# Block-granular projection items and a cost budget for interleaving them, in a cross-shaped window attention kernel

## The chip, the cores and the metric

The kernel runs on one core of one Trainium2 chip. The metric is the device time of one execution, in microseconds (us), as a median of several.

Engine names: PE is TensorE, ACT is ScalarE, DVE is VectorE, SP is the engine that issues most DMAs (all but three of those listed for the kernel before). "PEld" in profile lines is PE's weight load, which overlaps its matmuls (in the kernel before 575.6 us of it and 1049.5 us of matmuls lie in a span of 1307.2 us).

## The reference, cut to what matters

```python
qkv = einsum('bhwc,cd->bhwd', x, wqkv)           # x: 1 x 224 x 224 x 96, bf16
q, k, v = qkv[..., :96], qkv[..., 96:192], qkv[..., 192:]
# channels 0..47:  attention inside 28 horizontal windows, each 8 rows  x 224 columns
# channels 48..95: attention inside 28 vertical windows,   each 224 rows x 8 columns
ah = softmax(einsum('bqc,bkc->bqk', qh, kh) * 48 ** -0.5)
oh = einsum('bqk,bkc->bqc', ah, vh)              # and the same for qv, kv, vv
return einsum('bhwc,cd->bhwd', concat(oh, ov), wo)
```

There are 56 windows of 1792 tokens each, with head size 48. Phase one of the kernel does the 28 horizontal windows and phase two the vertical ones. Phase two also transposes and projects the result, so it has more work per window.

## The kernel before

A window's scores are cut into 25 groups. A group is up to 1024 columns of transposed scores: two PE matmuls of 512 columns side by side on two halves of the array (the pair takes 0.39 us, one projection of 512 columns 0.38), one exponential on ScalarE, and eight 49-column matmuls that multiply by V. The last group of a window is half-size (512 columns). Two groups make a *slot*: PE issues two scores groups and two V groups, and in what is left of the slot it works off a queue of *items* for the next window and the finished ones. Items are: `xt` (transpose x, four blocks), `k` and `q` (a projection of 512 columns), `v`, `ot` (transpose the attention output) and `fin` (final projection). Every item ends in a VectorE copy out of PSUM.

```python
def emit_from(maxn):                       # take up to maxn items that may start by now
    n = 0
    i = 0
    while n < maxn and i < len(queue):
        if queue[i][2] <= cur_slot["G"]:
            ent = queue.pop(i)
            _emit_entry(ent)
            n += 1
        else:
            i += 1
    return n
...
def enqueue_proj(wid, prologue=False):
    if prologue:
        order = [("xt", 0), ("k", 0), ("q", 0), ("xt", 1), ("v", 0), ("k", 1), ("xt", 2), ("k", 2), ...]
    else:
        order = [("xt", 0), ("xt", 1), ("k", 0), ("xt", 2), ("q", 0), ("k", 1), ("xt", 3), ("k", 2), ...]
...
# emit_st: scores of group G, into one of two PSUM buffers
if G >= 2:
    pe.wait(act, act_cnt[G - 2])
...
# main loop, even G: emit_st(G), then the V matmuls of G-3 and G-2, then items
gl = G % NGW                               # NGW = 25 groups per window
even_left = max(1, (NGW - gl + 1) // 2)
nelig = sum(1 for ent in queue if ent[2] <= G)
k = (nelig + even_left - 1) // even_left   # spread what is left over the slots left
k = max(1, min(3, k))
emit_from(k)
```

In front of the loop, eight warm-up matmuls of zeros are issued. The stores of the last window all go out on SP.

The softmax here doesn't subtract the row's maximum and nothing guards it: scores larger than these inputs give would overflow.

Of the kernel before, what the change touches and what calls it, by code (L numbers as in the profile page):

```python
# [8 lines left out]
BF16 = mybir.dt.bfloat16  # L9
F32 = mybir.dt.float32  # L10

KNOBS = dict(nwh=28, nwv=28, warm=8, dummies=0)


class _Prog:
# [38 lines left out]
def bass_standalone__window_attn_cswin__vision_kernel(nc, x, wqkv, wo, out):  # L54
# [12 lines left out]
    NGW = 25  # L67
# [8 lines left out]
    with ExitStack() as es:  # L76
# [40 lines left out]
        ohw_sem = [_DmaSem(sem("s_ohw%d" % s)) for s in range(2)]  # L117
        ldoh_sem = [_DmaSem(sem("s_ldoh%d" % s)) for s in range(2)]
        ost_sem = [_DmaSem(sem("s_ost%d" % s)) for s in range(2)]
        rq_sem = _DmaSem(sem("s_rq"))  # L120

        def dma(prog, dsem, out_ap, in_ap):
# [158 lines left out]
            misc_state["dve_hist"].append(c_dve)  # L281
            misc_state["n"] += 1

        def item_xt(wid, n):
            wd = wins[wid]
            s = wd["xs"]
            b = wd["b"]
            bank = misc_bank()
            pe.wait(pool, c_ident)
            q0, wdt = chunks[n]  # L290
            nb = wdt // 128
            dsem, cl = wd["c_ld"][n]
            pe.wait(dsem, cl)
            for bb in range(nb):
                blk = 4 * n + bb
                c = pe.op(lambda e, bb=bb, blk=blk, bank=bank, s=s: e.transpose(  # L296
                    psb[0:96, 1024 * bank + 128 * bb: 1024 * bank + 128 * (bb + 1)], xin[s][:, blk, :], ident[:, :]),
                    sig=(bb == nb - 1))
            wd["c_proj_pe_last"] = c
            dve.wait(pe, c)  # L300
            if wid >= NB:
                dve.wait(pe, wins[wid - NB]["c_proj_pe_last"])
            cd = dve.op(lambda e, bank=bank, b=b, q0=q0, wdt=wdt: e.tensor_copy(  # L303
                xT[b][:, q0:q0 + wdt], psb[0:96, 1024 * bank: 1024 * bank + wdt]), sig=True)
            wd["c_xt_dve"][n] = cd
            misc_done(cd)

        def xt_needed(wd, col0, ncol):
            ns = range(col0 // 512, (col0 + ncol - 1) // 512 + 1)
            return max(wd["c_xt_dve"][n] for n in ns)  # L310

        def item_qk(wid, n, which):
            wd = wins[wid]
            b = wd["b"]
            ph = wd["phase"]
            q0, wdt = chunks[n]
            bank = misc_bank()
            pe.wait(dve, xt_needed(wd, q0, wdt))
            pe.wait(pool, c_pool_const)
            if ph == 0:  # L320
                if which == "k":
                    pe.wait(w0_sem, c_wk0)
                    pe.wait(dve, c_wk0d)
                else:
                    pe.wait(w0b_sem, c_w0b)
                    pe.wait(dve, c_wq0d)
            else:
                pe.wait(w1_sem, cw1["c"])
            wmat = wq[ph] if which == "q" else wk[ph]
            c = pe.op(lambda e, bank=bank, b=b, q0=q0, wdt=wdt, wmat=wmat: e.matmul(  # L330
                ps[:, 512 * bank: 512 * bank + wdt], wmat[:, :], xT[b][:, q0:q0 + wdt], start=True, stop=True), sig=True)
            wd["c_proj_pe_last"] = c
            dst = QT[b] if which == "q" else KT[b]
            dve.wait(pe, c)
            if wid >= NB:
                assert wins[wid - NB]["n_st"] == NGW
                dve.wait(pe, wins[wid - NB]["c_st_last"])
            cd = dve.op(lambda e, bank=bank, dst=dst, q0=q0, wdt=wdt: e.tensor_copy(  # L338
                dst[:, q0:q0 + wdt], ps[:, 512 * bank: 512 * bank + wdt]), sig=True)
            (wd["c_q_dve"] if which == "q" else wd["c_k_dve"])[n] = cd  # L340
            misc_done(cd)

        def item_v(wid, n):
            wd = wins[wid]
            b = wd["b"]
            ph = wd["phase"]
            blk0, nb = (0, 8) if n == 0 else (8, 6)
            bank = misc_bank()
            pe.wait(dve, xt_needed(wd, 128 * blk0, 128 * nb))
            pe.wait(pool, c_pool_const)  # L350
            if ph == 0:
                pe.wait(w0b_sem, c_w0b)
            else:
                pe.wait(w1_sem, cw1["c"])
            for bb in range(nb):
                c = pe.op(lambda e, bank=bank, b=b, blk0=blk0, bb=bb, ph=ph: e.matmul(  # L356
                    ps[:, 512 * bank + 48 * bb: 512 * bank + 48 * (bb + 1)],
                    xT[b][:, 128 * (blk0 + bb): 128 * (blk0 + bb + 1)], wv[ph][:, :],
                    start=True, stop=True), sig=(bb == nb - 1))
            wd["c_proj_pe_last"] = c  # L360
            dve.wait(pe, c)
            if wid >= NB:
                assert wins[wid - NB]["n_pv"] == NGW
                dve.wait(pe, wins[wid - NB]["c_pv_last"])
            cd = dve.op(lambda e, bank=bank, b=b, blk0=blk0, nb=nb: e.tensor_copy(  # L365
                VA[b][:, blk0: blk0 + nb, 0:48], ps[:, 512 * bank: 512 * bank + 48 * nb].rearrange("p (a c) -> p a c", c=48)), sig=True)
            wd["c_v_dve"][n] = cd
            misc_done(cd)

        def item_ot(wid, j):  # L370
# [44 lines left out]
        def item_fin(wid, j):  # L415
# [29 lines left out]
                sp.wait(dsem, cprev)  # L445
            last_win = (w == NWV - 1)
            if last_win:
                for qb in range(nqb):
                    qbi = 4 * j + qb
                    dst = out[0, 16 * qbi:16 * qbi + 16, 8 * w:8 * w + 8, :].rearrange("r j c -> r (j c)")  # L450
                    c = rq_dma(dst, out_sb[vb][:, qbi, :])
                wd["c_ost"][j] = (rq_sem, c)
            else:
                dst = out2[w, q0:q0 + wdt, :].rearrange("(a p) c -> p a c", p=128)
                c = dma(sp, ost_sem[vb], dst, out_sb[vb][:, 4 * j:4 * j + nqb, :])
# [9 lines left out]
            fn()  # L465
            emitted.add(key)

        def emit_from(maxn):
            n = 0
            i = 0  # L470
            while n < maxn and i < len(queue):
                if queue[i][2] <= cur_slot["G"]:
                    ent = queue.pop(i)
                    _emit_entry(ent)
                    n += 1
                else:
                    i += 1
# [15 lines left out]
                pos += 1  # L493
            queue.insert(pos, [key, fn, not_before])

        def mk(kind, wid, n):
            if kind == "xt":
                return lambda: item_xt(wid, n)
            if kind == "k":
                return lambda: item_qk(wid, n, "k")  # L500
            if kind == "q":
                return lambda: item_qk(wid, n, "q")
            if kind == "v":
                return lambda: item_v(wid, n)
            raise ValueError(kind)

        def enqueue_proj(wid, prologue=False):
            if prologue:
                order = [("xt", 0), ("k", 0), ("q", 0), ("xt", 1), ("v", 0), ("k", 1), ("xt", 2), ("k", 2),
                         ("xt", 3), ("k", 3), ("v", 1), ("q", 1), ("q", 2), ("q", 3)]  # L510
            else:
                order = [("xt", 0), ("xt", 1), ("k", 0), ("xt", 2), ("q", 0), ("k", 1), ("xt", 3), ("k", 2),
                         ("v", 0), ("k", 3), ("v", 1), ("q", 1), ("q", 2), ("q", 3)]
            for kind, n in order:
                queue.append([(kind, wid, n), mk(kind, wid, n), 0])

        groups = []
        for wid, wd in enumerate(wins):
# [25 lines left out]
        def emit_st(G):  # L544
# [2 lines left out]
            b = wd["b"]  # L547
            q0, wdt = chunks[g["j"]]
            for (i, bk, col, width, rt) in g["tiles"]:
                ensure(("k", g["wid"], i // 4))  # L550
            ensure(("q", g["wid"], g["j"]))
            if G >= 2:
                pe.wait(act, act_cnt[G - 2])
            for (i, bk, col, width, rt) in g["tiles"]:
                pe.wait(dve, wd["c_k_dve"][i // 4])
            pe.wait(dve, wd["c_q_dve"][g["j"]])
            base = 1024 * (G % 2)
            nt = len(g["tiles"])
            for ti, (i, bk, col, width, rt) in enumerate(g["tiles"]):
# [21 lines left out]
        def emit_pv(G):  # L581
# [5 lines left out]
            q0c, wdtc = chunks[j]  # L587
            obank = 4 + (j % 2)
            for (i, pcol, q0, width) in g["pieces"]:
                ensure(("v", wid, i // 8))  # L590
            pe.wait(act, act_cnt[G])
            pe.wait(pool, c_pool_const)
            for (i, pcol, q0, width) in g["pieces"]:
                pe.wait(dve, wd["c_v_dve"][i // 8])
            if g["first_of_chunk"] and len(norm_hist) >= 2:
                pe.wait(dve, norm_hist[-2])
            pt = PT[G % NPT]
# [18 lines left out]
        def emit_norm(wid, j, c_pv):  # L616
# [42 lines left out]
                    else:  # L659
                        pending_hwin.append(wid)  # L660
            else:
                nb_ot = max(G + 2, wd.get("g_ldoh", 0) + KNOBS.get("oh_delay", 12))
                enqueue_prio(("ot", wid, j), (lambda wid=wid, j=j: item_ot(wid, j)), nb_ot)
                enqueue_prio(("fin", wid, j), (lambda wid=wid, j=j: item_fin(wid, j)), nb_ot + 2)

        pe.wait(pool, c_warm)
        for i in range(KNOBS["warm"]):
# [27 lines left out]
        while True:  # L695
# [12 lines left out]
            if G % 2 == 0 or G >= NG:  # L708
                for Gp in (G - 3, G - 2):
                    if 0 <= Gp < NG and Gp not in pv_cnt:  # L710
                        emit_pv(Gp)
                if G < NG:
                    gl = G % NGW
                    even_left = max(1, (NGW - gl + 1) // 2)
                    nelig = sum(1 for ent in queue if ent[2] <= G)
                    k = (nelig + even_left - 1) // even_left
                    k = max(1, min(3, k))
                else:
                    k = 2
                emit_from(k)  # L720
            G += 1
            if G >= NG + 4 and not queue:
                break
# [2 lines left out]
        flush_pending_out()  # L726
        flush_pending_hwin()
        sp.wait(rq_sem, rq_sem.cnt)

        @block.sync  # L730
        def _(e):
# [45 lines left out]
```

## Time and profile before

| | before |
|---|---|
| median time | 1312.21 us (4 runs, 1309.11 to 1313.8) |
| span of the profiled run (the fastest of the four) | 1307.2 us |
| ScalarE busy | 1272.7 us (97%) |
| ScalarE idle | 34.5 us |

The busy line of the page and its costliest group, of the kernel before. The group's columns are: line, engine, operation, tiles, count, busy us, mean ns of one, and the idle time in front of them with what ended it.

```profile
PE 1049.5 (80%) x16920; PEld 575.6 (44%) x16920; DVE 591.4 (45%) x1458; ACT 1272.7 (97%) x1401; POOL 1.8 (0%) x19
...
L571 ACT ACTIVATE PT<-ps 128x1024 bf16<-128x1024 f32 x1344 | 1244.1, 1079 | 25.2 <-PE ps L560 25.2
```

ScalarE is the limit. A change that leaves the exponentials alone can only win from its 34.5 us of idle time: 6.5 us before the first exponential (the table load, 1.28 us, is not counted), 20.9 us in gaps between exponentials, and 7.1 us after the last. In each gap ScalarE waits for PE's scores matmul (L560).

Where the gaps are is seen in ScalarE's timeline of the kernel before. Columns: start us, length us, engine, line, what, and in brackets the idle time in front and what ended it. The first lines are from phase one, the later ones from phase two.

```profile
268.19 0.78 ACT L573 ACTIVATE PT<-ps 128x512 bf16<-128x512 f32 x1
268.97 22.13 ACT L571 ACTIVATE PT<-ps 128x1024 bf16<-128x1024 f32 x24
290.80 0.80 ACT L573 ACTIVATE PT<-ps 128x512 bf16<-128x512 f32 x1
291.59 1.02 ACT L571 ACTIVATE PT<-ps 128x1024 bf16<-128x1024 f32 x1
292.89 21.19 ACT L571 ACTIVATE PT<-ps 128x1024 bf16<-128x1024 f32 x23 [0.27 <-PE ps L560]
313.79 0.78 ACT L573 ACTIVATE PT<-ps 128x512 bf16<-128x512 f32 x1
...
726.68 0.64 ACT L573 ACTIVATE PT<-ps 128x512 bf16<-128x512 f32 x1
727.48 22.20 ACT L571 ACTIVATE PT<-ps 128x1024 bf16<-128x1024 f32 x24 [0.16 <-PE ps L560]
...
751.46 21.21 ACT L571 ACTIVATE PT<-ps 128x1024 bf16<-128x1024 f32 x23 [0.27 <-PE ps L560]
772.52 0.64 ACT L573 ACTIVATE PT<-ps 128x512 bf16<-128x512 f32 x1
```

Read it by the half-size exponentials (L573), one per window. From one to the second next is 313.79 - 268.19 = 45.60 us in phase one and 772.52 - 726.68 = 45.84 us in phase two. Every second window has a gap of 0.27 us just behind its start, and in phase two the other windows have one of 0.16 us. This distance is *the length of a window pair*. It holds gaps too small to be listed, and it does not depend on the prologue or the tail.

The cause of the 0.27 us gap is in PE's timeline of the kernel before, at the same place:

```profile
291.16 0.39 PE L560 MATMUL ps<-QT,KT 49*128 49x512 bf16 x2 [0.61 <-ACT PT L571]
291.49 0.57 PE L606 MATMUL ps<-VA,PT 128*128 128x49 bf16 x16
291.90 0.63 PE L296 MATMUL ps<-ident,xin 128*96 128x128 bf16 x8
292.46 0.61 PE L560 MATMUL ps<-QT,KT 49*128 49x512 bf16 x4
```

The half-size exponential gives ScalarE less work (0.64 to 0.80 us, where full ones follow each other every 0.92), but this slot holds eight transposes. The scores at 292.46 come too late, and ScalarE waits until 292.89.

A second kind of gap comes at irregular places. For some microseconds all matmuls take longer, and the granted clock in the profile is then mostly 0.50 in place of 1.00 (it is 0.50 from 343 to 345 us in the kernel before, for one). This is called *half rate* below, and such a stretch a half-rate episode. In the kernel before, for example, a projection of 512 columns takes 0.60 us inside an episode and 0.38 us just behind it, and ScalarE has a gap of 0.62 us (lines of one timeline, others left out):

```profile
342.31 0.61 PE L560 MATMUL ps<-QT,KT 49*128 49x512 bf16 x2 [0.37 <-ACT PT L571]
343.52 0.60 PE L330 MATMUL ps<-xT,wq 96*128 96x512 bf16 x1
344.71 1.94 ACT L571 ACTIVATE PT<-ps 128x1024 bf16<-128x1024 f32 x2 [0.62 <-PE ps L560]
345.70 0.38 PE L330 MATMUL ps<-xT,wk 96*128 96x512 bf16 x1
```

### The profile page before, as it was taken

The numbers are of one execution on the slowest core, as the hardware profiler recorded it, in microseconds if no ns is written. First come the engines' busy times: TensorE is split into PE (matmuls) and PEld (weight loads), VectorE is DVE, ScalarE is ACT, GpSimd is POOL, SyncE is SP. The second block draws the span as 40 slices with busy tenths as digits, with TensorE's granted clock in tenths as the row PEclk, the third lists the DMA queues.
The fourth block names the chain that finished last, engine by engine and source line by source line (L and its number), as shares of the span: only waits on it lengthen the run. The fifth ranks groups of instructions, "written<-read, shape, count | busy, mean of one in ns | idle before, by whom it ended". The sixth has DMA issues, their size and how long they took to land.

```text
span 1307.2 us, 37524 instructions
## 1 busy us (share of the span) xinstructions
PE 1049.5 (80%) x16920; PEld 575.6 (44%) x16920; DVE 591.4 (45%) x1458; ACT 1272.7 (97%) x1401; POOL 1.8 (0%) x19
## 2 busy tenths in 40 slices
PE   7777877777777877777788888888888888888886
PEld 3444444444444444444444444444444444444443
DVE  3433434343343334434345555555555555555552
ACT  5999999999999999999999999999999999999997
POOL 0000000000000000000000000000000000000000
PEclk7999999999999999999999999999999999999999
DMA  1111111111111111111232222322232232223211
GB/s 38 46 50 40 43 51 46 50 47 42 44 46 52 46 51 38 45 50 46 53 62 48 61 49 54 60 52 56 49 62 49 52 61 54 55 46 66 49 42 30
DMA packets 194999, 64.78 MB, mean 50 GB/s; under 512 B 172408, under 2 KB 191384, under 8 KB 194840
## 3 DMA queue, kind: packets, MB, share of 16 engines
q1 hardware_dynamic: 194504, 62.37, 21.0%
q8 instruction: 132, 2.16, 0.7%
q14 instruction: 27, 0.22, 0.1%
q10 hardware_dynamic: 336, 0.03, 0.0%
HBM read 47.92 MB, written 38.19 MB: 66 GB/s over the span
## 4 chain that ended last, share of the span: by engine, by line
ACT 91%; PE 7%; DVE 1%; issue 0%; POOL 0%; POOLq 0%
ACT PT L571 91%; PE ps L560 3%; PE ps L606 2%; PE ps L296 1%; PE ps L383 1%; ACT PT L573 1%; PE ps L330 0%; PE ps L668 0%; DVE KT L338 0%; DVE xT L303 0%; DVE QT L338 0%; DVE out_sb L436 0%; PE ps L356 0%; DVE OTs L390 0%; PE ps L428 0%
## 5 line engine op out<-in xcount | busy, mean ns | idle before, releaser
L571 ACT ACTIVATE PT<-ps 128x1024 bf16<-128x1024 f32 x1344 | 1244.1, 1079 | 25.2 <-PE ps L560 25.2
L560 PE MATMUL ps<-QT,KT 49*128 49x512 bf16 (+1 forms) x3136 | 538.6, 362 | 247.6 <-ACT PT L571 241.4
L606 PE MATMUL ps<-VA,PT 128*128 128x49 bf16 x10976 | 399.5, 185 | 0.9 <-DVE VA L365 0.6
L606 PEld LDWEIGHTS ps<-VA,PT 128*128 128x128 bf16 x10976 | 323.6, 96 | 159.8 <-issue 155.2
L560 PEld LDWEIGHTS ps<-QT,KT 49*128 49x128 bf16 x3136 | 137.2, 93 | 555.9 <-ACT PT L571 490.5
L338 DVE CAST QT<-ps 128x512 bf16<-128x512 f32 x224 | 138.5, 619 | 108.2 <-PE ps L330 108.2
L338 DVE CAST KT<-ps 128x512 bf16<-128x512 f32 x224 | 138.4, 618 | 78.1 <-PE ps L330 78.1
L303 DVE COPY xT<-ps 96x512 bf16<-96x512 bf16 x224 | 83.2, 380 | 71.1 <-PE ps L296 71.0
L627 DVE RECIPROCAL rl<-ps 128x4 f32<-128x4 f32 x224 | 40.3, 180 | 162.5 <-PE ps L606 162.5
L390 DVE COPY OTs<-ps 96x512 bf16<-96x512 bf16 x112 | 43.3, 387 | 118.3 <-PE ps L383 118.3
L436 DVE CAST out_sb<-ps 128x384 bf16<-128x384 f32 x112 | 56.6, 506 | 82.1 <-PE ps L428 82.1
L365 DVE CAST VA<-ps 128x384 bf16<-128x384 f32 x112 | 56.4, 503 | 71.2 <-PE ps L356 71.2
L330 PE MATMUL ps<-xT,wk 96*128 96x512 bf16 x224 | 80.1, 358 | 1.4 <-DVE xT L303 1.4
L330 PE MATMUL ps<-xT,wq 96*128 96x512 bf16 x224 | 80.2, 359 | 0.0
L296 PE MATMUL ps<-ident,xin 128*96 128x128 bf16 x784 | 79.0, 224 | 0.0
L296 PEld LDWEIGHTS ps<-ident,xin 128*96 128x96 bf16 x784 | 58.7, 125 | 3.3 <-issue 0.5
L643 DVE TENSOR_TENSOR O_sb<-ps,rl 128x192 bf16<-128x192 f32 x112 | 37.3, 333 | 12.0 <-DVE rl L627 0.5
L383 PE MATMUL ps<-ident,Ocomb 128*96 128x128 bf16 x392 | 42.0, 224 | 0.0
L573 ACT ACTIVATE PT<-ps 128x512 bf16<-128x512 f32 x56 | 40.0, 715 | 0.0
L643 DVE TENSOR_TENSOR Ocomb<-ps,rl 128x192 bf16<-128x192 f32 x112 | 37.2, 332 | 3.9
L356 PE MATMUL ps<-wv,xT 96*128 96x48 bf16 x784 | 37.8, 184 | 0.5 <-DVE xT L303 0.5
L428 PE MATMUL ps<-wo_sb,OTs 96*128 96x96 bf16 x392 | 34.8, 205 | 1.0 <-DVE OTs L390 1.0
(23 smaller groups left out, 130.0 us busy)
## 6 DMA issues: line engine op xcount, KB each, us to landing
x_scratch<-in_x_dram SPq DMA_DIRECT2D x28, 336.0 KB
xin<-x_scratch SPq DMA_DIRECT2D x28, 336.0 KB, 3.7
xin<-in_x_dram SPq DMA_DIRECT2D x27, 336.0 KB, 3.0
out_dram<-out_scratch SPq DMA_DIRECT2D x27, 336.0 KB
out_scratch<-out_sb SPq DMA_DIRECT2D x81, 96.0 KB, 2.0
oh_scratch<-oh_scratch SPq DMA_DIRECT2D x28, 168.0 KB
Ocomb<-oh_scratch SPq DMA_DIRECT2D x28, 168.0 KB, 2.8
oh_scratch<-O_sb SPq DMA_DIRECT2D x84, 48.0 KB, 1.5
```

What stands on the lines that cost most here:

```text
L296: c = pe.op(lambda e, bb=bb, blk=blk, bank=bank, s=s: e.transpose(psb[0:96, 1024 * bank + 128 * bb: 1024 * bank + 128 * (bb + 1)], xin[s][ ...
L303: cd = dve.op(lambda e, bank=bank, b=b, q0=q0, wdt=wdt: e.tensor_copy(xT[b][:, q0:q0 + wdt], psb[0:96, 1024 * bank: 1024 * bank + wdt]), s ...
L330: c = pe.op(lambda e, bank=bank, b=b, q0=q0, wdt=wdt, wmat=wmat: e.matmul(ps[:, 512 * bank: 512 * bank + wdt], wmat[:, :], xT[b][:, q0:q0 ...
L338: cd = dve.op(lambda e, bank=bank, dst=dst, q0=q0, wdt=wdt: e.tensor_copy(dst[:, q0:q0 + wdt], ps[:, 512 * bank: 512 * bank + wdt]), sig=True)
L365: cd = dve.op(lambda e, bank=bank, b=b, blk0=blk0, nb=nb: e.tensor_copy(VA[b][:, blk0: blk0 + nb, 0:48], ps[:, 512 * bank: 512 * bank + 48 ...
L383: c = pe.op(lambda e, bank=bank, qb=qb, vb=vb, j=j: e.transpose(psb[0:96, 1024 * bank + 128 * qb: 1024 * bank + 128 * (qb + 1)], Ocomb[vb] ...
L436: cd = dve.op(lambda e, bank=bank, vb=vb, j=j, nqb=nqb: e.tensor_copy(out_sb[vb][:, 4 * j:4 * j + nqb, :], ps[:, 512 * bank: 512 * bank + ...
L560: c = pe.op(lambda e, base=base, bk=bk, col=col, width=width, rt=rt, i=i, b=b, q0=q0: e.matmul(ps[:, base + 512 * bk + col: base + 512 * b ...
L571: ca = act.op(lambda e, base=base, pt=pt: e.activation(pt[:, 0:1024], ps[:, base:base + 1024], ACTF.Exp, scale=scale), sig=True)
L573: ca = act.op(lambda e, base=base, pt=pt: e.activation(pt[:, 0:512].rearrange("p (b n) -> p b n", b=2), ps[:, base:base + 1024].rearrange( ...
L606: c = pe.op(lambda e, obank=obank, jj=jj, pt=pt, pcol=pcol, qb=qb, b=b, i=i, st=st: e.matmul(ps[:, 512 * obank + 64 * jj: 512 * obank + 64 ...
L643: c2 = dve.op(lambda e, so=so, nqb=nqb, oview=oview, dst=dst: e.tensor_tensor(dst, oview[:, :, 0:48], rl[so][:, 0:nqb].unsqueeze(2).broadc ...
```

## The change

The intent is to cut the queue's items by blocks of 128 columns, give each an estimated cost in ns, and let a slot take items only up to a budget: the slot's ScalarE time minus PE's fixed work. The prologue uses the finer items to start the first scores from half a projection, with fewer warm-ups. Rules for the last window are meant to shorten the tail. The core of the diff:

```diff
-KNOBS = dict(nwh=28, nwv=28, warm=8, dummies=0)
+KNOBS = dict(nwh=28, nwv=28, warm=3, dummies=0, oh_delay=12)
...
+                if j == 3:
+                    act.wait(dve, cd)
...
-                    c = rq_dma(dst, out_sb[vb][:, qbi, :])
+                    if j == 3:
+                        c = dma(act, fa_sem, dst, out_sb[vb][:, qbi, :])
+                    else:
+                        c = rq_dma(dst, out_sb[vb][:, qbi, :])
...
-        def emit_from(maxn):
+        def emit_from(maxn, budget=10 ** 9):
...
+                    cst = item_cost.get(queue[i][0], 200)
+                    if n > 0 and spent + cst > budget:
+                        break
+                    if n == 0 and cst > budget + 150:
+                        break
...
+            if prologue:
+                xt(0, 2); kq("k", 0, 256); xt(2, 2); kq("q", 0, 512); kq("k", 256, 256)
+                xt(4, 4); vv(0); kq("k", 512, 512); ...
...
-                nb_ot = max(G + 2, ...)
+                lastw = (w == NWV - 1)
+                nb_ot = max(G + (1 if lastw else 2), ...)
...
-                enqueue_prio(("fin", wid, j), ..., nb_ot + 2)
+                enqueue_prio(("fin", wid, j), ..., nb_ot + (1 if lastw else 2))
...
+                    period = 0
+                    for Gq in (G - 1, G):
+                        period += (458 if (... groups[Gq]["ncol"] == 512) else 916)
+                    npv = ...                      # V matmuls of this slot
+                    budget = period - 760 - (105 + 25 * npv)
...
+                    if lastw:
+                        k = 3
+                    emit_from(k, budget)
...
+            elif G < NG and groups[G]["wid"] == NWIN - 1 and G % NGW >= 20:
+                emit_from(1, 250)
```

Laid beside the kernel before, PE's instruction order differs in four places. The prologue's first three slots change. In phase one, half of the windows move four of eight transposes one slot on. In phase two about every second slot is filled differently. The fourth is the last window.

## The prediction

> **What bounds the kernel now.** The page's first part shows ScalarE busy 1272.7 of 1307.2 us (97%); the chain of waits is 91% its exponentials. They follow each other every 0.92 us (timeline: 23 in 21.19 us), and the change leaves their number and shape alone. So only ScalarE's 34.5 us of idle time can be won, 2.6% of the span.
>
> Where it is (ScalarE's waits and timeline):
> - start to first exponential at 7.78 us (1.28 us of it table load);
> - six more prologue gaps, 7.8 us together;
> - 0.27 us at the start of every second window, 28 times, 7.6 us;
> - 0.16 us in every second window of phase two, 14 times, 2.2 us;
> - 3 to 4 us where matmuls fall to half rate for a while in phase one (gaps of 0.3 to 1.1 us near 160, 200, 241, 344, 436, 476 us);
> - 7.1 us after the last exponential.
>
> **What the change does.** No arithmetic goes away. The instruction order shows:
>
> 1. *Phase one.* In 14 windows the slot after the half-size exponential held eight transposes; they now split 4 + 4 over two slots. Four take 0.24 us of PE pitch, so the next scores come that much earlier and the 0.27 us gap shrinks to about 0.03. The following slot had 0.28 us of PE waiting on ScalarE, so it can take the other four.
> 2. *Phase two.* The same slot held four output plus four input transposes; now only the output ones. The slot behind the 0.16 us gap loses a 256-column Q projection (about 0.2 us). The rest is a reshuffle with at most two items per slot, which never cost ScalarE anything at full rate before. Items 1 and 2: 28 x 0.24 + 14 x 0.16 = 8.9 us.
> 3. *Prologue.* The first K and transposes go in halves, and three warm-up matmuls remain of eight. But VectorE copies in order, behind a weight copy that waits for its DMA until 4.18 us[...]. [...] Net 0.3 us won.
> 4. *Last window.* The last two stores go out on ScalarE's queue instead of behind four others on SP's (six issues take 3.75 us): about 1.5 us won. Against it, twice an output transpose and its projection share a slot, and PE waits for the copy between them (0.92 us start to start at the trace's end): about 0.5 us of ScalarE idle each, 1.0 us lost.
>
> Sum: 8.9 + 0.3 + 1.5 - 1.0 = 9.7 us. The half-rate episodes should cost as before.
>
> **Predicted time: 1302.5 us**, 8 in 10 between 1298 and 1308. Faster by over 2%: 1%; within 2%: 98%; slower by over 2%: 1%.
>
> **What would show it.** ScalarE's wait on the scores falls from 25.2 us to about 17, from 53 waits to about 25; ScalarE busy unchanged at 1273 us; first exponential between 7.3 and 8.1 us; tail near 5.6 us; two new gaps near 0.5 us in the last window.
>
> **What would make it wrong.** More half-rate episodes, each up to 1 us, or fewer, if PE's load is spread differently. [...] Postponed items making VectorE hold the projection banks: new gaps in phase two.

The forecast's sum is 8.9 + 0.3 + 1.5 - 1.0 = 9.7 us, and 1312.2 - 9.7 = 1302.5 us.

## The result, and the profile after

The changed kernel's median is 1303.15 us (11 runs, 1300.67 to 1306.59), and that of before on the same chips 1312.95 us (16 runs). The ratio is 0.9927, with a 95% interval of 0.9914 to 0.994. Ratios here are the mean time of one kernel's fast runs over that of the other's of the same rounds, so they are not quite the ratio of the medians quoted.

The busy line and costliest group of the changed kernel. Its scores line is now L594, the exponential L605 and the half-size one L607.

```profile
PE 1055.8 (81%) x16916; PEld 578.1 (44%) x16916; DVE 591.6 (45%) x1460; ACT 1272.6 (98%) x1401; POOL 1.8 (0%) x19
...
L605 ACT ACTIVATE PT<-ps 128x1024 bf16<-128x1024 f32 x1344 | 1244.0, 1078 | 19.9 <-PE ps L594 17.9
```

ScalarE's work is the same. Its wait for the scores fell from 25.2 us to 17.9. Its timeline, in the same stretches:

```profile
265.38 0.78 ACT L607 ACTIVATE PT<-ps 128x512 bf16<-128x512 f32 x1
266.16 22.13 ACT L605 ACTIVATE PT<-ps 128x1024 bf16<-128x1024 f32 x24
287.99 0.79 ACT L607 ACTIVATE PT<-ps 128x512 bf16<-128x512 f32 x1
288.78 22.26 ACT L605 ACTIVATE PT<-ps 128x1024 bf16<-128x1024 f32 x24
310.75 0.78 ACT L607 ACTIVATE PT<-ps 128x512 bf16<-128x512 f32 x1
...
721.01 0.64 ACT L607 ACTIVATE PT<-ps 128x512 bf16<-128x512 f32 x1
721.69 22.14 ACT L605 ACTIVATE PT<-ps 128x1024 bf16<-128x1024 f32 x24
743.66 0.65 ACT L607 ACTIVATE PT<-ps 128x512 bf16<-128x512 f32 x1
744.31 22.31 ACT L605 ACTIVATE PT<-ps 128x1024 bf16<-128x1024 f32 x24
766.48 0.64 ACT L607 ACTIVATE PT<-ps 128x512 bf16<-128x512 f32 x1
```

No gap is listed. The window pair is 310.75 - 265.38 = 45.37 us in phase one and 766.48 - 721.01 = 45.47 us in phase two, 0.22 and 0.37 us shorter than before (most pairs of phase one took 45.59 us there, 0.01 less than the one shown). Over 14 pairs each, that is 3.1 + 5.2 = 8.3 us. PE, at the same place as before:

```profile
288.35 0.39 PE L594 MATMUL ps<-QT,KT 49*128 49x512 bf16 x2 [0.61 <-ACT PT L605]
288.67 0.57 PE L640 MATMUL ps<-VA,PT 128*128 128x49 bf16 x16
289.09 0.40 PE L296 MATMUL ps<-ident,xin 128*96 128x128 bf16 x4
289.42 0.83 PE L594 MATMUL ps<-QT,KT 49*128 49x512 bf16 x4
290.19 0.47 PE L640 MATMUL ps<-VA,PT 128*128 128x49 bf16 x12
290.50 0.40 PE L296 MATMUL ps<-ident,xin 128*96 128x128 bf16 x4
290.74 0.38 PE L331 MATMUL ps<-xT,wk 96*128 96x512 bf16 x1
291.05 0.39 PE L594 MATMUL ps<-QT,KT 49*128 49x512 bf16 x2
```

From the first scores to the next is 289.42 - 288.35 = 1.07 us; before it was 1.30. The other four transposes sit in the next slot and hold nobody up.

But the last window has become worse. ScalarE's timeline of the changed kernel there, down to its two stores:

```profile
1281.00 3.77 ACT L605 ACTIVATE PT<-ps 128x1024 bf16<-128x1024 f32 x4 [1.67 <-PE ps L594]
1284.96 1.94 ACT L605 ACTIVATE PT<-ps 128x1024 bf16<-128x1024 f32 x2 [0.20 <-PE ps L594]
1288.28 3.77 ACT L605 ACTIVATE PT<-ps 128x1024 bf16<-128x1024 f32 x4 [1.38 <-PE ps L594]
1292.24 1.94 ACT L605 ACTIVATE PT<-ps 128x1024 bf16<-128x1024 f32 x2 [0.20 <-PE ps L594]
1294.07 0.60 ACT L607 ACTIVATE PT<-ps 128x512 bf16<-128x512 f32 x1
1298.12 1.39 ACTq L126 DMA_DIRECT2D out_dram<-out_sb  x2
```

These are 3.45 us of gaps that the kernel before did not have in its profile. The tail from the end of the last exponential to the end of the span is 1301.6 - 1294.67 = 6.9 us, against 7.1 us before. The first exponential starts at 7.84 us (7.78 before). The unbroken run of exponentials that follows the prologue starts at 24.29 us (24.48 before).

### The profile page after: what moved, and what is told of

It is laid out like the page before. It is cut to its first block, busy times and chain, and to the rows that moved or that the text cites. A ratio compares the mean times of both kernels' runs of the same rounds, so it can differ in the third digit from the quotient of the medians.

```text
span 1301.6 us, 37519 instructions
## 1 busy us (share of the span) xinstructions
PE 1055.8 (81%) x16916; PEld 578.1 (44%) x16916; DVE 591.6 (45%) x1460; ACT 1272.6 (98%) x1401; POOL 1.8 (0%) x19
## 4 chain that ended last, share of the span: by engine, by line
ACT 91%; PE 8%; DVE 1%; issue 0%; DMA 0%; ACTq 0%
ACT PT L605 90%; PE ps L594 3%; PE ps L640 3%; PE ps L386 1%; ACT PT L607 1%; PE ps L296 0%; PE ps L331 0%; DMA wv<-in_wqkv_dram 0%; DVE KT L339 0%; PE ps L431 0%; DVE QT L339 0%; DVE OTs L393 0%; DVE xT L304 0%; DVE VA L367 0%; DVE out_sb L439 0%
## 5 line engine op out<-in xcount | busy, mean ns | idle before, releaser
L605 ACT ACTIVATE PT<-ps 128x1024 bf16<-128x1024 f32 x1344 | 1244.0, 1078 | 19.9 <-PE ps L594 17.9
L594 PE MATMUL ps<-QT,KT 49*128 49x512 bf16 (+1 forms) x3136 | 545.3, 363 | 234.8 <-ACT PT L605 228.4
L594 PEld LDWEIGHTS ps<-QT,KT 49*128 49x128 bf16 x3136 | 137.3, 93 | 544.5 <-ACT PT L605 479.3
L339 DVE CAST KT<-ps 128x256 bf16<-128x256 f32 x225 | 138.7, 616 | 109.2 <-PE ps L331 109.2
L304 DVE COPY xT<-ps 96x256 bf16<-96x256 bf16 x225 | 84.3, 379 | 49.3 <-PE ps L296 49.3
L296 PE MATMUL ps<-ident,xin 128*96 128x128 bf16 x784 | 81.9, 225 | 0.1
L331 PE MATMUL ps<-xT,wk 96*128 96x256 bf16 x225 | 79.9, 355 | 2.2 <-DVE xT L304 2.2
L607 ACT ACTIVATE PT<-ps 128x512 bf16<-128x512 f32 x56 | 39.6, 708 | 0.0
```

Of the source, the lines that this page charges most:

```text
L296: c = pe.op(lambda e, bb=bb, blk=blk, bank=bank, s=s: e.transpose(psb[0:96, 1024 * bank + 128 * bb: 1024 * bank + 128 * (bb + 1)], xin[s][ ...
L304: cd = dve.op(lambda e, bank=bank, b=b, q0=q0, wdt=wdt: e.tensor_copy(xT[b][:, q0:q0 + wdt], psb[0:96, 1024 * bank: 1024 * bank + wdt]), s ...
L331: c = pe.op(lambda e, bank=bank, b=b, q0=q0, wdt=wdt, wmat=wmat: e.matmul(ps[:, 512 * bank: 512 * bank + wdt], wmat[:, :], xT[b][:, q0:q0 ...
L339: cd = dve.op(lambda e, bank=bank, dst=dst, q0=q0, wdt=wdt: e.tensor_copy(dst[:, q0:q0 + wdt], ps[:, 512 * bank: 512 * bank + wdt]), sig=True)
L594: c = pe.op(lambda e, base=base, bk=bk, col=col, width=width, rt=rt, i=i, b=b, q0=q0: e.matmul(ps[:, base + 512 * bk + col: base + 512 * b ...
L605: ca = act.op(lambda e, base=base, pt=pt: e.activation(pt[:, 0:1024], ps[:, base:base + 1024], ACTF.Exp, scale=scale), sig=True)
```

## The experiments

Two theories are tested. **Theory S**: the gain is PE work taken out of the two crowded slots. **Rivals**: the gain is fewer stretches in which matmuls run at half rate (R), or it comes from the prologue and the tail (E). The first job was one set of four on one chip, and so were the second and the third; the column of before is that of the same set. In all of them before is the kernel before, without fillers.

| run | median us (lowest to highest) | before, same chip | ratio, 95% interval |
|---|---|---|---|
| a_budget_only | 1301.12 (1298.76 to 1302.9) | 1313.8 | 0.9903 (0.9887 to 0.9919) |
| b_ends_only | 1315.53 (1313.63 to 1316.81) | 1313.8 | 1.0012 (0.9996 to 1.0029) |
| c_last_window_off | 1300.86 (1297.64 to 1302.71) | 1313.8 | 0.9897 (0.9879 to 0.9915) |
| d_warm8 | 1304.08 (1302.2 to 1305.24) | 1313.8 | 0.9927 (0.9911 to 0.9942) |
| e_before_filled | 1305.74 (1304.6 to 1311.35) | 1312.75 | 0.996 (0.9942 to 0.9978) |
| f_after_filled | 1298.38 (1297.57 to 1300.03) | 1312.75 | 0.9893 (0.988 to 0.9906) |
| g_budget_filled | 1296.77 (1296.59 to 1298.19) | 1312.75 | 0.9882 (0.9869 to 0.9894) |
| h_prologue_filled | 1306.97 (1305.41 to 1308.32) | 1312.75 | 0.9961 (0.9948 to 0.9974) |
| i_filled_store | 1296.44 (1295.5 to 1302.47) | 1314.39 | 0.9865 (0.9845 to 0.9886) |
| j_filled_store_halves | 1296.54 (1296.36 to 1296.62) | 1314.39 | 0.9866 (0.9847 to 0.9886) |
| k_budget_filled_again | 1297.51 (1296.63 to 1298.11) | 1314.39 | 0.9873 (0.9853 to 0.9893) |
| l_prologue_full_rows | 1296.17 (1296.13 to 1301.74) | 1314.39 | 0.9874 (0.9849 to 0.9899) |

All twelve gave correct results.

### a_budget_only: the budget without the ends

```diff
 (against the changed kernel)
-                xt(0, 2); kq("k", 0, 256); xt(2, 2); kq("q", 0, 512); kq("k", 256, 256)
+                xt(0, 4); kq("k", 0, 512); kq("q", 0, 512)
-KNOBS = dict(..., warm=3, ...)
+KNOBS = dict(..., warm=8, ...)
-                lastw = (w == NWV - 1)
+                lastw = False               # both places; the extra odd-slot emit removed too
-                    c = dma(act, fa_sem, ...)   # j == 3
+                    c = rq_dma(...)             # all stores on SP again
```

> The changed kernel with the prologue, the eight warm-ups, the last window and the stores of the kernel before; only the cost budget remains. Theory S (slots): the gain is the PE work taken out of the two crowded slots behind each half-size exponential, so this alone wins 8 to 9 us (ratio to before about 0.9935), ScalarE's small regular gaps of 0.27 and 0.16 us are gone, and the distance from one half-size exponential to the second next is 45.4 us in phase one (45.6 before) and 45.5 in phase two (45.8 before). Rival R (rate): the gain is only that fewer half-rate episodes of the matmuls occur; then the regular gaps stay near 0.27 us and the ratio moves with the granted clock. Rival E (ends): the gain is in the prologue and the tail; then this shows about 0.

It won 12.7 us (1313.8 to 1301.12), which is more than the whole change. Its undisturbed window pairs are 45.37 and 45.47 us, and after the prologue its profile lists only four gaps, in three places, none of them at the old spots in the windows' rhythm. So theory S holds for the regular gaps and E falls. But 12.7 is more than the 8.3 us that the regular gaps explain. The rest has to come from something that is not in every window.

### b_ends_only: the ends without the budget

```diff
-                    emit_from(k, budget)
+                    emit_from(k, 10 ** 9)
```

> The other half: prologue by halves, three warm-ups, last-window rules and ScalarE-queue stores, but no budget (its limit is set to infinity). Theory S: the crowded slots are back, about 42 regular gaps; the ends cost as much as they win, so within 3 us of before, rather slower: -3 to +1 us gained (the trace of the changed kernel shows 3.45 us of new ScalarE gaps in the last window against 0.2 us won in the prologue and 0.2 in the tail). Rival E: faster by most of the 9.7 us.

The ratio, 1.0012, is not told from 1 by its interval. The profile shows the regular gaps again: 0.27 us in 26 places, the 0.16 us ones, window pairs of 45.59 and 45.83 us. It also has the 1.67 and 1.38 us gaps of the last window. The budget-only kernel and this one together are the whole change, and their ratios multiply to 0.9915, just inside the interval of the change itself (0.9914 to 0.994).

### c_last_window_off: no special rules for the last window

```diff
-                lastw = (w == NWV - 1)
+                lastw = False
-                    lastw = (groups[G]["wid"] == NWIN - 1)
+                    lastw = False
-            elif G < NG and groups[G]["wid"] == NWIN - 1 and G % NGW >= 20:
-                emit_from(1, 250)
```

> The changed kernel with the last-window rules off: an output transpose and its final projection are again two slots apart; budget, prologue and ScalarE-queue stores stay. Theory: the 1.67 and 1.38 us gaps of the last window come from the PE waiting for VectorE's copy inside one slot; they vanish, and the time falls by 2 to 3.5 us below the changed kernel (about 1300.5). Rival: they come from the matmuls at half rate in the last window (they were at half rate from 1277.5 us on); then gaps of 0.2 to 1 us remain whenever the clock is low, and the time falls by under 1 us.

It is 3.2 us faster than d_warm8, which keeps those rules and ran beside it; up to 0.9 us of that can be the later start that d's eight warm-ups gave it (below). Against the changed kernel itself, which ran in another set, the ratios to before differ by 0.003, or 3.9 us. In its profile the last window ran at half rate too (four transposes took 0.64 us), and still the gaps there sum to 1.4 us (0.17, 0.63, 0.59) in place of 3.45. The listed gaps are not the whole loss, though: the last window pair took 45.27 us in a, 48.09 in c and 49.35 in the changed kernel. So both are at work, and in these two profiles half rate costs more (2.8 us) than the rules add to it (1.3 us). The stall inside one slot is a fault of the rules, and at half rate its gap is longer (0.58 and 1.60 us in d, below). My expectation that the gaps would vanish was wrong, because the half rate came without the rules as well. The rules may also bring the half rate on. Of the profiles with the rules, the changed kernel and d have four transposes in 0.64 us there, the half-rate time, and b and f have gaps of the same length (1.67 and 1.38 us, 1.40 us). Without the rules c, e and i have the 0.64 us, and before and g have a clock of 1.00 there. That is a count, not a test.

### d_warm8: eight warm-ups again

```diff
-KNOBS = dict(..., warm=3, ...)
+KNOBS = dict(..., warm=8, ...)
```

> The changed kernel with eight warm-up matmuls again. Theory W: the three warm-ups left the first projections at half rate (256 columns took 0.40 us, 512 took 0.58); with eight, the first exponential starts at 7.3 to 7.5 us in place of 7.84 and the time falls by about 0.4 us. Rival: VectorE's weight copy, waiting for its DMA until 4.25 us, holds the first chain; then under 0.15 us.

No gain. In this profile the eight warm-ups held the first transposes until 4.76 us (2.96 in the changed kernel), and the first projections were at half rate all the same (512 columns took 0.59 us). The first exponential started at 8.74 us. The run also separates the two costs of the last window. ScalarE's lines of d_warm8 there:

```profile
1281.46 5.68 ACT L605 ACTIVATE PT<-ps 128x1024 bf16<-128x1024 f32 x6 [0.58 <-PE ps L594]
1288.74 3.77 ACT L605 ACTIVATE PT<-ps 128x1024 bf16<-128x1024 f32 x4 [1.60 <-PE ps L594]
```

And PE's transposes and projections in front of these two gaps:

```profile
1279.83 0.40 PE L386 MATMUL ps<-ident,Ocomb 128*96 128x128 bf16 x4
1280.75 0.34 PE L431 MATMUL ps<-wo_sb,OTs 96*128 96x96 bf16 x4 [0.52 <-DVE OTs L393]
...
1286.50 0.64 PE L386 MATMUL ps<-ident,Ocomb 128*96 128x128 bf16 x4
1287.66 0.50 PE L431 MATMUL ps<-wo_sb,OTs 96*128 96x96 bf16 x4 [0.52 <-DVE OTs L393]
```

PE waits 0.52 us for the same VectorE copy both times. At full rate (four transposes in 0.40 us) ScalarE's gap is 0.58 us. At half rate (0.64 us) it is 1.60 us, because PE's other work in the slot takes longer: from the scores in front of the first stall to the next scores it is 1.93 us in d (1279.09 to 1281.02, full rate), and 2.80 us in the changed kernel (1277.55 to 1280.35, half rate).

### e_before_filled, f_after_filled, g_budget_filled: the same three kernels with fillers

Fillers are matmuls of zeros into unused PSUM columns. They change no result.

```diff
         def emit_dummies(G):                # runs in front of the scores of an even G
-            nd = KNOBS["dummies"]
-            if nd <= 0 or ...
+            nd = {0: 4, 1: 2}.get(fill["n"], 0)   # by the items of the slot just before
+            if G < 24 or nd <= 0 or ...
                 # nd matmuls, 49 rows x 256 columns of zeros
-                emit_from(k)
+                fill["n"] = emit_from(k)
```

> The kernel before with filler matmuls of zeros (256 columns, two in front of a slot that follows a slot with one projection item, four after one with none), from the first window on, to keep PE from falling to half rate. The budget alone won 12.7 us against 8.3 us that its regular gaps explain (14 window pairs x 0.22 us in phase one, 14 x 0.37 us in phase two, read from the distance of half-size exponentials). Theory H: the other 4 us are half-rate episodes, which cost the kernel before more. Then this wins 3 to 5 us over before, its granted clock is 0.985 or more (before 0.965 to 0.988), and its window pairs stay at 45.59 and 45.83 us with no longer ones among them. Rival: the fillers only take PE time, no gain or a loss, and the clock stays near 0.977.

> The changed kernel with the same fillers. Theory H: the half-rate episodes go, so 2 us from the middle, and in the last window the two stalls cost 0.6 us each in place of 1.67 and 1.38, so another 1.5 to 2 us: about 1299.5 us, ratio to before about 0.990. The distance to the filled kernel before shrinks to the regular gaps minus the last window, about 7 us. Rival: no change against the changed kernel (0.9927).

> The budget alone with the same fillers. Theory H: against the filled kernel before the difference is the regular gaps only, 8.3 us (7.5 to 9), in place of the 12.7 us without fillers; about 1299.5 us. Window pairs all at 45.37 and 45.46 us. Rival: it keeps a distance of 12 us to the filled kernel before; then the budget's extra 4 us are not a matter of the clock.

The fillers alone win 7 us on the kernel before (1312.75 to 1305.74), more than the 3 to 5 us expected, although PE does more. All window pairs of phase one but the first are then 45.59 or 45.60 us; without fillers, six of the thirteen pairs in the profile were 46.24 to 46.42. In four of its six runs the filled kernel before took 1305.3 us on average, with a granted clock of 0.991 or 0.992. In the other two, at 0.981, it took 1311.3; one of these is the profiled one, and its last window is at half rate (four transposes in 0.64 us) with 4 us of gaps. Against those four runs the filled budget kernel (mean 1297.1) is 8.3 us faster, which is just the 8.3 us of the regular gaps. The four were chosen after the fact, by their clock; the medians of all runs are 9.0 us apart. So most or all of the extra 4 us that the budget wins without fillers is half-rate time, and rival R is right about a third of its gain. The profiles without fillers point the same way: the longer pairs of before add 4.3 us, those of a (two of them) 1.8 us.

The granted clock points the same way for these kernels, which share prologue and warm-ups: its median is 0.977 to 0.979 for before, 0.985 for the budget alone, and 0.992 for the budget with fillers. An estimate from that: if every loss of clock is time at 0.50, as in the episode at 343 us, the time at half rate is twice the lost share, some 55 to 60 us per run in before, 39 with the budget and 21 with fillers too. Some 17 us of each is the prologue (mean clock 0.66 in its 24.5 us in the profile of before). The record is weak evidence for a single run: of the runs of a, the slowest (1302.9 us) had the highest clock, 0.992. It can also be wrong: in the changed kernel it says 1.00 from 11 to 22 us, where pairs of 512-column scores took 0.61 us, the half-rate time. So mean clocks are compared here only between kernels with the same eight warm-ups, and even there one can mislead: the profiled run of k has 0.999, though its first projections took 0.61 and 0.63 us.

The filled change is 1.6 us slower than the filled budget (1298.38 against 1296.77). That is what the ends still cost, net of what store and prologue win, when the clock is mostly kept; in its profile the two stalls of the last window were 0.58 and 1.40 us, the second near the 1.38 to 1.67 us seen at half rate. Both f and g came out under the 1299.5 us that was expected of each.

### h_prologue_filled and l_prologue_full_rows: fillers in the prologue

```diff
 (against g_budget_filled)
+            if wid == 0:
+                prologue_dummies(2)         # in front of each K or Q projection of window 0
             pe.wait(dve, xt_needed(wd, q0, wdt))
+            if G <= 12:
+                prologue_dummies(5 if G == 0 else 3)   # in front of the scores
 (l_prologue_full_rows against h_prologue_filled)
-                    ps[:, ...], warm[0:49, 0:128], warm[0:49, 0:256],
+                    ps[:, ...], warm[:, 0:128], warm[:, 0:256],
```

> The budget with fillers, and fillers in the first 13 groups too, at the points where PE waits for VectorE. Theory: the prologue's gaps (16.5 us from the first exponential to the one at about 24.5 us, of which 10 are work) are lengthened by the half rate that holds there until 23 us; at full rate PE's chain of projections is shorter and 1.5 to 3 us come off. Rival: the gaps are set by VectorE's copies (0.69 us each, two in a row) and the fillers only delay PE: no gain or a loss of about 1 us.

> The prologue with fillers again, which lost 9 us because PE stayed at half rate from 11 to 34 us although it was busy 97% of that time. The fillers now use all 128 rows of the array in place of 49. Theory A: what raises the rate is how much of the array works, not how long PE is busy; then the rate is full before 16 us and the loss shrinks to 3 us or less. Rival: rows do not matter, PE stays at half rate until after 30 us again and the loss stays near 9 us.

The first lost: it was 10.2 us slower than the same kernel without prologue fillers. The second, with full rows, lost nothing: three of its four runs took 1296.13 to 1296.19 us, 1.3 us under the yardstick k of the same chip, and the fourth 1301.74 us, so the mean says nothing. The profiles say more than the times. First the stretch from 12 to 24 us of h_prologue_filled. Columns: stretch, length, busy us of each engine with its instruction count, granted clock, DMA share, GB/s.

```profile
12.00:24.00 12.00, 11.45 (x80) 5.29 (x79) 2.98 (x7) 4.78 (x5) 0.00 (x0) 0.50 0.00 1
```

The same stretch of l_prologue_full_rows:

```profile
12.00:24.00 12.00, 10.88 (x130) 6.03 (x128) 4.77 (x11) 7.49 (x8) 0.00 (x0) 1.00 0.02 5
```

A projection of 512 columns in h_prologue_filled, from PE's timeline:

```profile
13.05 0.61 PE L345 MATMUL ps<-xT,wk 96*128 96x512 bf16 x1
```

And the same one in l_prologue_full_rows:

```profile
13.24 0.39 PE L345 MATMUL ps<-xT,wk 96*128 96x512 bf16 x1 [0.30 <-DVE xT L304]
```

With 49-row fillers PE was busy 95% of the time, by the profile, and stayed at half rate (clock 0.50, the projection in 0.61 us). With 128-row fillers it was busy 91% and ran at full rate (1.00, 0.39 us). The only difference between the two programs is the rows, so theory A holds for this stretch. (That is one profile each, but the five runs of h all took over 7 us longer than any run of g.) It does not hold everywhere: the fillers of e and g also have 49 rows, and there, in the windows, the median clock rose with them all the same (0.979 to 0.991 in e).

The prologue itself became shorter, by less than the 1.5 to 3 us hoped for in h. From the first exponential to the first half-size one, which ends window 0, it took 29.28 us with full rows (8.50 to 37.78), 30.41 in g (7.80 to 38.21) and 30.94 in k (8.63 to 39.57). ScalarE's gaps in that stretch sum to 6.4 us in l, 7.8 in g and 8.2 in k. That is 1.1 to 1.7 us won, about what separates the times of l and k.

### k_budget_filled_again, i_filled_store, j_filled_store_halves: the two other ends

```diff
 (i against g: the stores of the change are kept)
-                    c = rq_dma(...)                  # j == 3
+                    c = dma(act, fa_sem, ...)
 (j against i: the prologue in halves and warm=3, as in the change)
```

> The budget with fillers again, unchanged, as the yardstick on the same chip for the other three: ratio to before 0.988, about 1297 us, no ScalarE gap after the prologue.

> The budget with fillers, plus one thing: the last two stores go out on ScalarE's queue instead of behind four others on SP's. The matmul order is the same, instruction by instruction, as in the budget with fillers, which runs beside it. My prediction: 1.5 us won; from the filled trace, where six issues follow each other every 0.6 us, two of them come forward by at most 1.2 us, so the tail after the last exponential should be 5.9 to 6.3 us in place of 7.1. Rival: the first four stores, and the time from the last issue to the end, hold the tail anyway; under 0.4 us won.

> As the run with fillers and the ScalarE store, plus the prologue of the change (first K and transposes in halves, three warm-ups). Theory: the halves bring the second exponential forward by 0.4 to 0.6 us and win 0.2 us at the end of the prologue; with the first exponential at the same time this is 0 to 0.3 us, not to be told from zero by times. Rival: the missing warm-ups keep the clock low for longer; 1 us or more lost.

Five of the six runs with the store took 1295.5 to 1297.4 us. The sixth, the profiled one, took 1302.47 and had its last window at half rate (four transposes in 0.64 us). The median of i is 1.1 us under that of k. With the halves too, the four runs lie within 0.3 us of each other and 1.0 us under k. By the times alone this is not clear: the runs of i and k overlap, the intervals of the ratios do too, and in k's profile the first exponential starts 0.8 us later than in that of g, the same program. The clear evidence is the tail after the last exponential: 6.2 us in j (1288.54 to 1294.7) and 7.1 us in g and k. The last window was alike in all three: from the half-size exponential near 1197 us to the end of the span it is 98.7 us in g, where the clock is 1.00 from 1270 to 1288 us, 98.7 in k, and 97.7 in j, just the tail's 0.9 less. So the store on ScalarE's queue wins 0.9 us, and the prologue by halves is not told from zero. (The expectation of k, no ScalarE gap after the prologue, holds but for one of 0.37 us at 27.73.) The 0.9 us fits the issue time: on SP six of these issues take 3.75 us in before, 0.6 each, and two of them, 1.2 us at most, were taken off the end.

## Why the prediction was right

The predicted 1302.5 us and the measured 1303.15 agree. The largest term, the regular gaps, was right in mechanism and size. That the total agrees to 0.65 us is partly luck: two other terms were off by some 4 and 2 us, in opposite directions.

1. **Regular gaps, predicted 8.9 us: measured 8.3 us.** Shown by the window pairs and by e against g. The gaps shrank by 0.22 us in phase one, where 0.24 was predicted, and by 0.37 us for the two in phase two, where 0.40 was predicted. The mechanism is shown: PE's time to the next scores fell by as much (1.30 to 1.07 us in phase one).
2. **"The half-rate episodes should cost as before": wrong by about 4 us.** The budget reduced them (granted clock 0.977 to 0.985) and won 12.7 us in place of 8.3. Both numbers are from the budget alone; in the changed kernel itself this term was not measured apart. Why the new order keeps the rate better is not shown. In the prologue the rate followed the rows in use (clock 0.50 in h, 1.00 in l), but no run here tells which slots count in the windows.
3. **Last window, predicted 1.0 us lost: measured 2.3 to 3.9 us lost** (c against d and against the changed kernel). The mechanism, an output transpose and its projection in one slot with VectorE's copy between them, is shown by c and d. Its predicted size, 0.5 us each, is the full-rate size (0.58 us in d and f). What was missed is that PE ran at half rate in the last window of the changed kernel (clock 0.50 from 1277.5 to 1295 us) and in part of d's, and there the stall becomes 1.4 to 1.7 us; b and f have gaps of that length too. PE has less to do in that window (busy 73% of 1278 to 1300 us in before, 83% in the rest of phase two), but in before it stayed at full rate there (clock 1.00), and a has no gap there, so why it drops is not shown.
4. **Stores, predicted 1.5 us won: measured 0.9 us** (the tail of j against g and k). In the changed kernel itself only 0.2 us of it is seen, with PE at half rate (clock 0.55 from 1275 to 1301 us).
5. **Prologue, predicted 0.3 us won: 0 to 0.2 us.** VectorE took its copies in order, as predicted: in the changed kernel the first transposes end at 3.38 us, and their copy starts at 4.33, behind the weight copy at 4.25. With three warm-ups and the halves, the first exponential came between 7.77 and 8.26 us in five profiles (the changed kernel, b, c, f, j); the first Q projection of 512 columns took 0.58 us, the half-rate time, in the two whose start was looked at (the changed kernel and b). Eight warm-ups mostly went with full rate there: of nine profiles with them, six had that projection in 0.38 or 0.39 us (before, a, e, g, h, i), and three had not: d (0.59), k (0.63) and l (0.46). With the old prologue order, eight of them and no fillers in the prologue, the first exponential came at 7.66 to 8.20 us in the five profiles that had full rate (before, a, e, g, i) and at 8.63 in k, which had not.

Sum of the measured terms, a rough one: 8.3 + 4 + 0.9 + 0.1 - 3 = 10.3 us, against 9.8 us between the medians. Of the signs named in advance, ScalarE's busy time and the first exponential came as said, and so did its wait (17.9 us against about 17), though 3.45 us of that are the last window's. The count fell further than said (17 waits against "about 25"), and the two new gaps of the last window were three times as long. The tail was 6.9 us in place of 5.6. The store explains 0.6 us of that miss (6.2 in j); in i, with the store but at half rate (four transposes in 0.64 us), the tail is 6.6 us, so half rate may account for a part of the rest.

What beats both kernels: the budget, fillers, the store on ScalarE's queue and no last-window rules (i and j), at about 1296.5 us. The budget with fillers alone (g) is within 1 us of that, and l, without the store but with full-row fillers in the prologue, had three runs at 1296.2; l's fillers and the store were not tried together.

## What to carry to other kernels

When one engine is 97% busy, add up its idle time by place before and after. Here a change won 12.7 us in the middle and gave back some 2 to 3 at the end, and the total alone would have hidden both. Count an interleaving slot in time, with the smaller slots counted as smaller: a rule that spreads items by number overfills just the half-size slot. And where PE is the engine that feeds the bottleneck, keep its rate in view: in the last window a stall of 0.58 us became 1.6 us when the matmuls ran at half rate.
